# A channel-mix weight stored by column group, so that each decoded set of parts is one contiguous run

## The chip, the cores and the metric

The kernel runs on one core of one Trainium2 chip. The metric is device time in microseconds (us): three runs of the kernel before gave 630.12 to 631.0 us, with a median of 630.76 us. A core has five engines that run side by side and each take their instructions in order: TensorE (PE, with PEld for loading its stationary operand), VectorE (DVE), ScalarE (ACT), GpSimd (POOL) and SyncE (SP), which here issues all the DMAs.

## The reference

For four batches of 768 tokens, three stages follow each other.

```python
# 1. a decayed scan over time, 8 heads of width 48 (384 channels)
y[:, :, t] = einsum(r_t, state + einsum(u * k_t, v_t)); state = w_t * state + einsum(k_t, v_t)
# 2. causal attention of 4 experts (width 64), every expert computed, the best two of a token mixed
a = softmax(scale * q @ k.T, causal); out += gate * (a @ v @ wo[e])
# 3. layernorm and channel mix, w_ch1: 384 x 1536, w_ch2: 1536 x 384
ch = maximum(xn @ w_ch1, 0) @ w_ch2; return x + ch
```

The weights arrive as 64-bit floats and have to become 16-bit pairs on the chip (a high part, and a low part that holds the rest), so that a product is three matmuls of 16-bit operands.

## The kernel before

The scan is worked in six chunks of 128 tokens for a batch (names `seq`, `bw`, `fw`, `k`, `rp`, `am`, and on PE `pk`, `pa`, `pcb`, `pd`, `py`), the attention in six query tiles (`pq`, `pv`, `ps`, the transposed probabilities `pt`, `po`, `oT`, `px`), and the channel mix in three groups of 256 tokens for a batch (`xnT`, `pm` at L1532 with w_ch1, `hid`, `pz` at L1565 with w_ch2). Scan of batch b+1, attention of batch b and channel mix of batch b-1 or b are interleaved.

Weight `w1` (the first channel-mix weight, 384 rows) is held in a tile `w_w` of 12 parts of 128 x 384; before, part `4*kk + f` holds rows 128*kk and on, of column group f (KK = 3 row blocks, 4 column groups). `w2` has 12 parts as well. The parts are fetched in *sets*: three parts of w1 (one column group) or two of w2. For each set:

- a DMA (L552) brings the 64-bit words into a raw tile (`x` for w1, `xnT` for w2);
- DVE decodes them in three instructions to 32-bit floats, written over the place in `w_w` where the 16-bit pairs will stand: L505 (one source: shift and mask), L506 and L507 (two sources: the sign, then the low bits);
- ACT squares and sums them (L575, `top`), for the scales.

From the first set's sum the scales follow, and then each part goes through PE, ACT, PE, ACT: a product with a diagonal matrix that scales it (L655, `times`), its 16-bit high part written to `w_w` (L659, `hi`), that part subtracted in the accumulator (L663, `less`), and the rest written as the low part (L667, `lo`). Later sets of w2 instead go over ACT L632 and DVE L636.

In the old layout the three parts of a w1 set stand four apart: parts f, 4+f, 8+f. The decode reads and writes `full[:, pick]` with a stride of four parts, so that from the set's first element to its last lie parts of other sets.

The order is not that of the source. Each step is recorded as an operation with an engine, a length and its dependencies; a planner then sorts the operations of each engine by due numbers (sums of entries of the table `PLACE` by group, step and index) and emits them in that order. Semaphore waits are added afterwards by the framework, from which ranges of a tile instructions read and write. A few filler matmuls (L744, `spin`) are put in by the planner near the start, where PE would stand idle.

Of the kernel before, what the change touches and what calls it, by code (L numbers as in the profile page):

```python
# [20 lines left out]
P = 128  # L21
# [5 lines left out]
KK = DM // P  # L27
# [10 lines left out]
PRM = dict(LOOK=0.0, LATE=1773.6262, UNTIL=43.8356, SPAN=6.2999, LEAST=0.0732, GAP=2.1085, LAND=2.27, NPA=6, NQ=1, NCB=8, DIRECT=('w2',), NST=10)  # L38
PLACE = {
# [21 lines left out]
    ('o', 3, 5): -698477.53, ('proj', 0): -295018.27, ('proj', 0, 's'): -125022.81, ('proj', 0, 1): 80220.25,  # L61
    ('proj', 0, 2): -21343.01, ('proj', 1): -177643.56, ('proj', 1, 1): -107377.99, ('proj', 1, 2): -196040.46,
    ('proj', 2): -91098.53, ('proj', 2, 1): 13642.21, ('proj', 2, 2): -449346.82, ('proj', 3): 93391.83,
# [12 lines left out]
    ('vals', 0, 1): 35417.3, ('vals', 0, 2): -24875.8, ('vals', 1): -89872.89, ('vals', 2): 21146.28,  # L76
# [7 lines left out]
    ('w2', 8): 67189.64, 'a_den': -27933.93, 'a_hi': -151558.33, 'a_lo': 225945.59, 'a_of': -8012.47,  # L84
    'a_sum': 90213.0, 'a_tr': -81147.68, 'ae': 9532.96, 'am_copy': 126573.78, 'f_flag': -83856.37,
    'f_rows': 359040.86, 'f_turn': 39994.68, 'f_w': 28227.87, 'forth': 248281.69, 'g_exp': 19442.15,
    'g_norm': -38900.58, 'g_peak': -151938.75, 'g_rank': 230355.43, 'hi': 134007.83, 'less': -136319.44,
    'lo': -225283.24, 'load': -122866.37, 'load_g': -30043.72, 'load_k': -57046.71, 'load_q': -279458.56,
    'load_r': -217492.83, 'load_u': -13561.36, 'load_ut': 56724.36, 'load_v': 141804.62, 'm_hi': -262991.62,
    'm_lo': 122988.52, 'm_out': -32307.81, 'm_store': 132697.31, 'mk': 33523.95, 'mk_begin': 34263.89,  # L90
    'mk_bonus': -306653.38, 'mk_cb': -154529.96, 'mk_dec': -93213.35, 'mk_diag': -197725.73, 'mk_k2': 294244.16,
    'mk_k2t': 81775.2, 'mk_rk': -143861.49, 'mk_rp': -291319.24, 'mk_ruk': -96442.3, 'mk_sd': -340521.47,
    'mk_side': 120524.29, 'mk_tot': 228284.39, 'mm_1': 319489.06, 'mm_2': 191970.76, 'mm_a': -77276.6,
    'mm_av': -163565.22, 'mm_cb': 11831.02, 'mm_d': -269837.93, 'mm_inter': -24853.46, 'mm_intra': -48830.3,
    'mm_k': -8197.28, 'mm_o': 142200.91, 'mm_q': -177202.8, 'mm_s': -59954.25, 'mm_v': -130717.65, 'mt': -15383.65,
    'n_hi': -5943.82, 'n_lo': -146399.19, 'n_root': -31312.6, 'n_tr': 121898.14, 'n_var': -147654.16,
    'n_xn': -111826.26, 'o1': 140934.93, 'o2': -234884.57, 'o3': 6748.89, 'o4': -239856.13, 'o5': 93661.14,
    'o_mean': 273629.77, 'o_st': 120380.94, 'o_x1': -222100.87, 'q_hi': 140529.69, 'q_less': 98224.57,
    'q_lo': 97584.28, 's_bias': -108185.03, 's_exp': 5623.4, 's_hi': 119074.81, 's_lo': 11657.8, 's_max': 72228.32,
    's_tr': 53618.26, 'scan': 180273.48, 'se': -288101.94, 'stack_k': 117902.0, 'stack_q': 35533.64,  # L100
    'state': -226076.38, 'times': 63945.68, 'top': 19104.78, 'unpack': -157479.11, 'unpack2': 157371.31,
    'unpack3': 101864.41, 'v_hi': 188866.74, 'v_lg': -140728.23, 'v_lo': 25317.14, 'vc': -144449.83,
    'w_check': 22598.42, 'w_sane': 282903.73, 'ws_hi': 30208.09, 'ws_less': -128406.54, 'ws_lo': -66728.24,
# [200 lines left out]
NR = KK * DF // RW  # L304
# [1454 lines left out]
```

## Time and profile before

| | before |
|---|---|
| median of three runs | 630.76 us (630.12 to 631.0) |
| the profiled execution | 629.59 us |
| its span | 627.3 us, 16254 instructions |
| mean granted TensorE clock | 0.970 |
| PE busy | 598.3 us (95%) |
| DVE, ACT, POOL busy | 427.4, 386.0, 140.1 us |

The 2.3 us between the profiled execution and its span lie around the span and are not seen in the trace. PE is the engine of which the most is used; a stretch of the span can shorten only where PE stands idle or runs at the lower of its two clocks (1.2 GHz, written 0.5, and 2.4 GHz, written 1.0), and the rows below are chosen to show where that is.

### The profile page before, as it was taken

The numbers are of one execution on the slowest core, as the hardware profiler recorded it, in microseconds if no ns is written. First come the engines' busy times: TensorE is split into PE (matmuls) and PEld (weight loads), VectorE is DVE, ScalarE is ACT, GpSimd is POOL, SyncE is SP. The second block draws the span as 40 slices with busy tenths as digits, with TensorE's granted clock in tenths as the row PEclk, the third lists the DMA queues.
The fourth block names the chain that finished last, engine by engine and source line by source line (L and its number), as shares of the span: only waits on it lengthen the run. The fifth ranks groups of instructions, "written<-read, shape, count | busy, mean of one in ns | idle before, by whom it ended". The sixth has DMA issues, their size and how long they took to land.

```text
span 627.3 us, 16254 instructions
## 1 busy us (share of the span) xinstructions
PE 598.3 (95%) x6593; PEld 440.9 (70%) x6594; DVE 427.4 (68%) x808; ACT 386.0 (62%) x1062; POOL 140.1 (22%) x176
## 2 busy tenths in 40 slices
PE   6589899899999999999999999999999999999996
PEld 3357566677668866876877676776886768687783
DVE  5978788988978588888874898674464555542220
ACT  5367889876765586776656777573464756343120
POOL 4613043333644034325400232000000000000000
PEclk8659999899999999999999999999999999999999
DMA  8623764698996488739754767626228454522000
GB/s 279 228 101 124 191 168 128 130 226 212 193 215 123 93 217 162 186 81 248 168 84 103 194 128 162 112 56 121 48 43 152 93 102 85 100 62 60 14 14 31
DMA packets 150706, 82.15 MB, mean 131 GB/s; under 512 B 123616, under 2 KB 136672, under 8 KB 150624
## 3 DMA queue, kind: packets, MB, share of 16 engines
q1 hardware_dynamic: 150624, 81.03, 56.5%
q8 instruction: 54, 0.88, 0.6%
q14 instruction: 28, 0.23, 0.1%
HBM read 41.16 MB, written 4.72 MB: 73 GB/s over the span
## 4 chain that ended last, share of the span: by engine, by line
PE 72%; ACT 12%; DVE 10%; issue 3%; DMA 2%; SPq 0%; POOL 0%; ACTq 0%; DVEq 0%
PE pz L1565 21%; PE pm L1532 18%; PE pq L1123 7%; PE ps L1302 5%; PE po L1387 4%; PE px L1439 3%; ACT ps L1344 3%; PE pa L918 3%; PE py L968 2%; PE py L954 2%; PE pv L1188 1%; PE pk L936 1%; ACT hl L1360 1%; PE pd L983 1%; DMA xnT<-in_w_dram 1%
## 5 line engine op out<-in xcount | busy, mean ns | idle before, releaser
L1565 PE MATMUL pz<-w_w,hid 128*128 128x384 f16 x864 | 151.0, 326 | 0.2 <-DVE hid L1547 0.2
L1532 PE MATMUL pm<-xnT,w_w 128*128 128x256 f16 x1296 | 149.9, 273 | 0.2 <-DVE hid L1547 0.2
L1532 PEld LDWEIGHTS <-w_w 128*128 128x128 f16 x1296 | 124.8, 98 | 17.1 <-issue 1.7
L1565 PEld LDWEIGHTS <-hid 128*128 128x128 f16 x864 | 81.9, 98 | 50.7 <-issue 1.8
L1364 DVE SCALAR_TENSOR_TENSOR hl<-ps,hl 128x512 f16<-128x512 f32 (+2 forms) x68 | 54.7, 812 | 33.7 <-ACT hl L1360 33.0
L1547 DVE SCALAR_TENSOR_TENSOR hid<-pm,hid 128x512 f16<-128x512 f32 x72 | 49.3, 687 | 37.7 <-ACT hid L1543 37.6
L1543 ACT ACTIVATE hid<-pm 128x512 f16<-128x512 f32 x72 | 42.8, 594 | 50.8 <-PE pm L1532 50.7
L1481 POOL TENSOR_TENSOR rs_y<-rs_v,half 128x2 f32<-128x2 f32 x12 | 9.4, 780 | 229.6 <-ACT rs_v L1477 229.6
L1123 PE MATMUL pq<-xT,w_qk 128*128 128x256 f16 x432 | 51.8, 273 | 0.5 <-ACT qs L1148 0.5
L1360 ACT ACTIVATE hl<-ps 128x512 f16<-128x512 f32 (+2 forms) x68 | 46.7, 696 | 4.9 <-DMA pt<-hl 3.6
L1344 ACT ACTIVATE ps<-ps,bias 128x640 f32<-128x640 f32 (+1 forms) x32 | 26.2, 820 | 37.1 <-DVE ps L1315 34.1
L1123 PEld LDWEIGHTS <-w_qk 128*128 128x128 f16 x432 | 41.7, 98 | 6.9 <-issue 1.3
L891 POOL TENSOR_SCALAR_AFFINE_SELECT am<-cb 128x512 f32<-128x512 f32 x48 | 34.7, 745 | 40.2 <-DVE cb L877 26.2
L833 POOL TENSOR_TENSOR rp<-seq,fw 128x512 f32<-128x512 f32 x24 | 30.6, 1273 | 51.0 <-DVE fw L816 42.5
L1387 PEld LDWEIGHTS <-pt 128*128 128x128 f16 x1008 | 37.2, 99 | 5.6 <-DMA pt<-hl 1.0
L1387 PE MATMUL po<-vt,pt 128*128 128x64 f16 x1008 | 40.3, 194 | 0.6 <-DMA pt<-hl 0.5
L1572 DVE SCALAR_TENSOR_TENSOR x<-pz,ioutFalse,x 128x384 f32<-128x384 f32 x24 | 14.7, 614 | 36.7 <-PE pz L1565 36.7
L1315 DVE TENSOR_SCALAR_CACHE_REDUCE ps<-ps,scales 128x640 f32<-128x640 f32 (+1 forms) x32 | 30.6, 956 | 12.8 <-PE ps L1305 12.7
L1344 ACT ACTIVATE ps<-ps,bias,scales 128x128 f32<-128x128 f32 (+3 forms) x64 | 37.9, 591 | 1.8
L925 DVE COPY_PREDICATED am<-above,pa 128x512 f32<-128x512 int8 x48 | 33.0, 723 | 4.3 <-PE pa L918 4.2
L801 DVE TENSOR_TENSOR_SCAN bw<-seq,starts 128x516 f32<-128x516 f32 x24 | 30.9, 1288 | 1.5 <-DMA seq<-in_seq_dram 1.5
L918 PE MATMUL pa<-rp,k 48*128 48x128 f32 x384 | 29.6, 290 | 1.7 <-DVE dec L996 1.6
(225 smaller groups left out, 1060.0 us busy)
## 6 DMA issues: line engine op xcount, KB each, us to landing
seq<-in_seq_dram SPq DMA_DIRECT2D x48, 256.0 KB, 4.0
seq<-in_seq_dram SPq DMA_DIRECT2D x24, 258.5 KB, 3.3
tok<-in_tok_dram SPq DMA_DIRECT2D x16, 384.0 KB, 4.0
seq<-in_seq_dram SPq DMA_DIRECT2D x24, 192.0 KB, 4.0
xnT<-in_w_dram SPq DMA_DIRECT2D x6, 768.0 KB, 4.4
x<-in_w_dram SPq DMA_DIRECT2D x4, 1152.0 KB, 7.2
out_dram<-x SPq DMA_DIRECT2D x24, 192.0 KB, 2.6
xk<-kd SPq DMA_DIRECT2D x16, 192.0 KB, 4.2
```

Of the source, the lines that this page charges most:

```text
L891: G.affine_select(out=t["am"][:, j], in_=t["cb"].rearrange("p (h j) -> p h j", j=2)[:, :, j, None].to_broadcast([P, NP, P]), compare_op=OP ...
L918: T.matmul(t["pa"][j][:, hp * P : (hp + 1) * P], t["k2"][o : o + D, hp, :], t["rp"][o : o + D, hp, :], start=True, stop=True)
L925: V.copy_predicated(t["am"][:, j], above[:, None, :].to_broadcast([P, NP, P]), t["pa"][j].rearrange("p (h t) -> p h t", t=P))
L1123: T.matmul(h["pq"][:, :n].rearrange("p (c t) -> p c t", t=P), wt["qk"][:, lw, kk, mt * P : (mt + 1) * P], t["xT", c0 // 2][:, :, lx * KK + ...
L1344: A.activation(ps, ps, AF.Exp, bias=h["bias"][:, e : e + 1], scale=-1.0 if alone else t["x"]["esc"], accum_out=r["sums"][:, e : e + 1])
L1360: A.activation(part(u, heads, 0, W), view(heads, h, W, spot), AF.Copy, scale=2.0 ** 14)
L1364: V.scalar_tensor_tensor(out=part(u, heads, half_at, W), in0=view(heads, h, W, spot), scalar=2.0 ** 14, in1=part(u, heads, 0, W), op0=OP.m ...
L1387: T.matmul(r["po"][:, e * HD : (e + 1) * HD], u["pt"][:, (lp * len(heads) + k) * (i + 1) + kb, :], t["vt"][:, kb, lv, e * HD : (e + 1) * H ...
L1532: T.matmul(h["pm"][:, j * 256 : (j + 1) * 256].rearrange("p (c t) -> p c t", t=P), wt["w1"][:, 4 * kk + f // 3, lw, f % 3 * P : (f % 3 + 1 ...
L1543: A.activation(hid[fp][:, 0], h["pm"], AF.Relu)
L1547: V.scalar_tensor_tensor(out=hid[fp][:, 1], in0=h["pm"], scalar=0.0, in1=hid[fp][:, 0], op0=OP.max, op1=OP.subtract)
L1565: T.matmul(h["po"][:, :DM], hid[fp][:, lh, c0 : c0 + P], wt["w2"][:, 2 * fp + j, lw, :], start=(fp + j + i == 0), stop=(fp == NF // 2 - 1 ...
```

## The change

The parts of w1 are renumbered: part `KK*f + kk` now holds row block kk of column group f, so that the three parts of a set are neighbours. The decode's view of the tile becomes one run of 1152 elements; the DMA still fetches the same strided columns from the weight. Who indexes the tile by part is changed to match. Beside that the whole table of due numbers is set anew, of which two lines stand here.

```diff
-PRM = dict(LOOK=0.0, LATE=1773.6262, UNTIL=43.8356, SPAN=6.2999, LEAST=0.0732, GAP=2.1085, ...)
+PRM = dict(LOOK=0.0, LATE=4084.3652, UNTIL=54.3975, SPAN=7.4609, LEAST=0.218, GAP=1.7191, ...)
 PLACE = {
-    ('av', 0, 0): 47055.04, ('av', 0, 1): -203728.69, ('av', 0, 2): -46772.52, ('av', 0, 3): -134002.41,
+    ('av', 0, 0): 16836.1, ('av', 0, 1): -209210.03, ('av', 0, 2): -42671.94, ('av', 0, 3): -81935.9,
...
-    SETS = dict(w1=[[4 * kk + f for kk in range(KK)] for f in range(4)], w2=[[2 * j, 2 * j + 1] for j in range(NR // 2)])
+    SETS = dict(w1=[[KK * f + kk for kk in range(KK)] for f in range(4)], w2=[[2 * j, 2 * j + 1] for j in range(NR // 2)])
...
-                pick = slice(some[0], some[-1] + 1, some[1] - some[0])
+                pick = slice(some[0], some[-1] + 1)
+                src = slice(k, None, 4) if which == "w1" else pick
...
-                def load(pick=pick, flat=flat, ring=ring, hold=hold, n=n, direct=direct):
+                def load(pick=src, flat=flat, ring=ring, hold=hold, n=n, direct=direct):
...
-                    kk = part * KK // NR
+                    kk = part % KK
...
-                    T.matmul(hold["ps"], diags[which][:, part * KK // NR if which == "w1" else 0], full[:, part], start=True, stop=True)
+                    T.matmul(hold["ps"], diags[which][:, part % KK if which == "w1" else 0], full[:, part], start=True, stop=True)
...
-                @op("PE", 0.98, after=[q["ready"]] + [big_done["w1"][4 * kk + (2 * fp + j) // 3] for kk in range(KK)], follow=[mms[-1] if mms else pe],
+                @op("PE", 0.98, after=[q["ready"]] + [big_done["w1"][KK * ((2 * fp + j) // 3) + kk] for kk in range(KK)], follow=[mms[-1] if mms else pe],
...
-                                     wt["w1"][:, 4 * kk + f // 3, lw, f % 3 * P : (f % 3 + 1) * P], q["xnT"][:, :, lx * KK + kk, :],
+                                     wt["w1"][:, KK * (f // 3) + kk, lw, f % 3 * P : (f % 3 + 1) * P], q["xnT"][:, :, lx * KK + kk, :],
```

What the planner makes of it shows at three places. The lines of the changed kernel are one higher from L546 on.

On DVE, at the decode of the second set of w1 (`w_w_132` is w1, `w_w_133` w2, `x_69` and `xnT` their raw tiles), before:

```order
L505 TENSOR_SCALAR w_w_132<-x_69 128x3x384
L713 SCALAR_TENSOR_TENSOR w_vg<-raw_vg_165,s_all_False,w_vg 128x4
L506 SCALAR_TENSOR_TENSOR w_w_132<-x_69,w_w_132 128x3x384
L507 SCALAR_TENSOR_TENSOR w_w_132<-x_69,w_w_132 128x3x384
L506 SCALAR_TENSOR_TENSOR w_w_133<-xnT,w_w_133 128x768
```

and of the changed kernel at the same place:

```order
L505 TENSOR_SCALAR w_w_132<-x_69 128x1152
L714 SCALAR_TENSOR_TENSOR w_vg<-raw_vg_165,s_all_False,w_vg 128x4
L506 SCALAR_TENSOR_TENSOR w_w_132<-x_69,w_w_132 128x1152
L507 SCALAR_TENSOR_TENSOR w_w_132<-x_69,w_w_132 128x1152
L506 SCALAR_TENSOR_TENSOR w_w_133<-xnT,w_w_133 128x768
```

Nothing moved here; the written piece became one run.

On PE, where the fourth query tile of batch 0 is multiplied out (`po_3`, its third piece reading `pt_3_2`), before:

```order
L1532 MATMUL pm_0_4_1994<-xnT,w_w_132 128x256
L1387 LDWEIGHTS pt_3_2_1925
L1387 MATMUL po_3_1854<-vt_715,pt_3_2_1925 128x64
...
L1387 MATMUL po_3_1854<-vt_715,pt_3_2_1925 128x64
L979 MATMUL pd_2_2022<-dec_102,ident 128x384
L983 MATMUL pd_2_2022<-seq_2_1666,k2t_2_1989 48x48 x8
L1387 LDWEIGHTS pt_3_3_1953
```

and now:

```order
L1533 MATMUL pm_0_4_1998<-xnT,w_w_132 128x256
L980 MATMUL pd_2_2014<-dec_102,ident 128x384
L984 MATMUL pd_2_2014<-seq_2_1670,k2t_2_1993 48x48 x8
L1388 LDWEIGHTS pt_3_2_1929
L1388 MATMUL po_3_1858<-vt_719,pt_3_2_1929 128x64
```

The nine `pd_2` matmuls moved from behind the third piece of `po_3` to ahead of it.

On SP's queue, at the last query tile of batch 1 (`pt_5_...` are transposes of its probabilities, `seq_3` and `tok_3` the inputs of a scan chunk of batch 3), before:

```order
L1373 DMA_TRANSPOSE pt_5_1_4778<-hl_5_1_4740 128x12x128
L1373 DMA_TRANSPOSE pt_5_2_4857<-hl_5_2_4819 128x12x128
L1428 DMA_TRANSPOSE oT_4_4888<-o_1_4_4754 128x4x128
L1373 DMA_TRANSPOSE pt_5_3_4935<-hl_5_3_4908 128x12x128
L1428 DMA_TRANSPOSE oT_5_5056<-o_1_5_5045 128x4x128
```

and now:

```order
L1374 DMA_TRANSPOSE pt_5_1_4788<-hl_5_1_4744 128x12x128
L773 DMA seq_3_4883<-in_seq_dram 128x517
L797 DMA tok_3_4891<-in_tok_dram 128x768
L1374 DMA_TRANSPOSE pt_5_2_4896<-hl_5_2_4847 128x12x128
L781 DMA seq_3_4883<-in_seq_dram 128x512
L785 DMA seq_3_4883<-in_seq_dram 128x512
L1429 DMA_TRANSPOSE oT_4_4928<-o_1_4_4754 128x4x128
L789 DMA seq_3_4883<-in_seq_dram 128x384
L1374 DMA_TRANSPOSE pt_5_3_4975<-hl_5_3_4941 128x12x128
```

Five input loads moved from behind the whole tile to between its transposes. From here to the attention of batch 3 the orders of PE, ACT, DVE and SP differ in many places; ahead of here they differ in few.

## Rows read from the trace of the kernel before

**Rows 1.** The head of the page.
```profile
span 627.3 us, 16254 instructions
```

**Rows 2.** Stretches: us, busy PE, PEld, DVE, ACT, POOL (count), clock, DMA, GB/s.
```profile
0.00:45.00 45.00, 30.38 (x213) 18.50 (x215) 35.29 (x79) 22.61 (x78) 19.94 (x31) 0.66 0.59 195
45.00:150.00 105.00, 97.21 (x1135) 69.08 (x1134) 90.49 (x164) 87.83 (x260) 31.75 (x35) 0.98 0.69 171
150.00:615.00 465.00, 463.61 (x5207) 349.21 (x5204) 300.40 (x564) 275.52 (x726) 88.38 (x111) 1.00 0.56 118
```

**Rows 3.** Line 505: duration min/median/max in ns, first and last start, forms.
```profile
L505 DVE TENSOR_SCALAR w_w<-xnT x6: 551/627/984, 15.1 to 111.1; 128x768 int32<-128x768 int32 x6
L505 DVE TENSOR_SCALAR w_w<-x x4: 1340/1344/1348, 21.2 to 74.3; 128x1152 int32<-128x1152 int32 x4
```

**Rows 4.** Timeline of the second w1 set: start, length, instruction, [idle before, releaser].
```profile
34.80 1.19 POOL L833 TENSOR_TENSOR rp<-seq,fw 128x512 f32<-128x512 f32 x1 [4.09 <-DVE fw L816]
...
35.42 1.34 DVE L505 TENSOR_SCALAR w_w<-x 128x1152 int32<-128x1152 int32 x1
...
37.45 1.35 DVE L506 SCALAR_TENSOR_TENSOR w_w<-x,w_w 128x1152 int32<-128x1152 int32 x1
38.09 1.06 PE L725 MATMUL ws_ps<-raw_qk,sd 128*128 128x256 f32 x2
...
38.89 0.49 ACT L659 ACTIVATE w_w<-w_ps_False 128x384 f16<-128x384 f32 x1 [0.76 <-DVE w_w L506]
...
39.42 1.36 DVE L507 SCALAR_TENSOR_TENSOR w_w<-x,w_w 128x1152 int32<-128x1152 int32 x1 [0.62 <-ACT w_w L659]
...
40.83 0.48 PE L663 MATMUL w_ps_False<-w_w,minus 128*128 128x384 f16 x1 [1.68 <-DVE w_w L507]
```

**Rows 5.** Pieces of the chain that ended last: start, length, what.
```profile
41.31 1.44 PE py L968 x24
...
43.17 1.27 PE w_ps_False L655 x2
...
54.45 0.79 PE py L968 x24
...
88.07 0.65 PE w_ps_False L655 x2
```

**Rows 6.** Busy time and granted clock in four short stretches, columns as in rows 2.
```profile
39.00:41.00 2.00, 0.32 (x2) 0.00 (x0) 1.58 (x2) 0.66 (x2) 0.00 (x0) 0.50 0.00 0
...
44.00:45.00 1.00, 0.55 (x3) 0.15 (x2) 0.00 (x0) 0.47 (x2) 0.00 (x0) 1.00 0.76 262
113.00:115.00 2.00, 0.43 (x7) 0.46 (x9) 1.95 (x5) 1.98 (x4) 0.00 (x0) 1.00 1.03 202
116.00:119.00 3.00, 3.00 (x30) 2.37 (x28) 3.00 (x4) 3.00 (x8) 0.72 (x1) 0.50 0.56 190
```

**Rows 7.** Timeline at the fourth w1 set, columns as in rows 4.
```profile
75.69 0.49 ACT L659 ACTIVATE w_w<-w_ps_False 128x384 f16<-128x384 f32 x1 [0.66 <-PE py L954]
...
77.78 0.32 PE L663 MATMUL w_ps_False<-w_w,minus 128*128 128x384 f16 x1 [0.19 <-DVE w_w L506]
...
79.24 0.49 ACT L1002 ACTIVATE spare<-py 128x384 fp8e4<-128x384 f32 x1
```

**Rows 8.** Timeline at the third w1 set, POOL beside DVE.
```profile
54.80 2.34 POOL L891 TENSOR_SCALAR_AFFINE_SELECT am<-cb 128x512 f32<-128x512 f32 x2
54.93 1.71 DVE L506 SCALAR_TENSOR_TENSOR w_w<-x,w_w 128x1152 int32<-128x1152 int32 x1
```

**Rows 9.** PE's waits up to 150 us: us in total, times, longest.
```profile
PE po L1387 <- DMA pt<-hl: 0.5, 1, 0.5
```

**Rows 10.** The tile `pt`, written by transposing DMAs: time to landing.
```profile
DMA to landing us min/median/max: 3.0/3.8/6.5
```

**Rows 11.** Timeline at the end of batch 1's last query tile.
```profile
325.11 1.42 SPq L1373 DMA_TRANSPOSE pt<-hl  x1
...
330.14 0.70 PE L1387 MATMUL po<-vt,pt 128*128 128x64 f16 x18
```

More of the change, by code (lines that the diff above doesn't have):

```diff
@@ L36 @@
 PACK = OFF_TV + DM
-PRM = dict(LOOK=0.0, LATE=1773.6262, UNTIL=43.8356, SPAN=6.2999, LEAST=0.0732, GAP=2.1085, LAND=2.27, NPA=6, NQ=1, NCB=8, DIRECT=('w2',), NST=10)
+PRM = dict(LOOK=0.0, LATE=4084.3652, UNTIL=54.3975, SPAN=7.4609, LEAST=0.218, GAP=1.7191, LAND=2.27, NPA=6, NQ=1, NCB=8, DIRECT=('w2',), NST=10)
 PLACE = {
[21 rows of a table removed]
-    ('o', 3, 5): -698477.53, ('proj', 0): -295018.27, ('proj', 0, 's'): -125022.81, ('proj', 0, 1): 80220.25,
-    ('proj', 0, 2): -21343.01, ('proj', 1): -177643.56, ('proj', 1, 1): -107377.99, ('proj', 1, 2): -196040.46,
-    ('proj', 2): -91098.53, ('proj', 2, 1): 13642.21, ('proj', 2, 2): -449346.82, ('proj', 3): 93391.83,
[12 rows of a table removed]
-    ('vals', 0, 1): 35417.3, ('vals', 0, 2): -24875.8, ('vals', 1): -89872.89, ('vals', 2): 21146.28,
[7 rows of a table removed]
[L84 to L103, printed above, removed]
-    'ws_load': 66852.66, 'ws_times': -17374.3, 'ws_top': -348457.17, 'x_hi': -14285.97, 'x_lo': 26889.45,
-    'x_rest': -61247.9, 'xabs': -182346.53,
[21 rows of a table added]
+    ('o', 3, 5): -702290.43, ('proj', 0): -300762.99, ('proj', 0, 's'): 3258.44, ('proj', 0, 1): 93098.76,
+    ('proj', 0, 2): -21532.93, ('proj', 1): -194846.79, ('proj', 1, 1): -182281.63, ('proj', 1, 2): -206567.32,
+    ('proj', 2): -139967.36, ('proj', 2, 1): -60620.28, ('proj', 2, 2): -471991.76, ('proj', 3): 33470.28,
[12 rows of a table added]
+    ('vals', 0): -221914.55, ('vals', 0, 1): 9510.27, ('vals', 0, 2): -3038.04, ('vals', 1): -123387.73,
[8 rows of a table added]
+    'a_hi': -190161.82, 'a_lo': 255406.1, 'a_of': -1740.35, 'a_sum': 77515.98, 'a_tr': -87884.88, 'ae': 27221.68,
+    'am_copy': 109115.04, 'f_flag': -61865.24, 'f_rows': 383190.12, 'f_turn': 50312.51, 'f_w': 27951.92,
+    'forth': 229228.26, 'g_exp': 45423.87, 'g_norm': -61796.84, 'g_peak': -154339.3, 'g_rank': 221135.62,
+    'hi': 130307.72, 'less': -133603.61, 'lo': -226558.93, 'load': -122063.24, 'load_g': -63513.62,
+    'load_k': -47163.22, 'load_q': -260808.06, 'load_r': -213091.8, 'load_u': -988.12, 'load_ut': 54846.76,
+    'load_v': 150565.96, 'm_hi': -311237.37, 'm_lo': 98927.68, 'm_out': 48881.52, 'm_store': 128283.34,
+    'mk': 37503.41, 'mk_begin': 79557.08, 'mk_bonus': -282399.21, 'mk_cb': -133359.0, 'mk_dec': -110093.06,
+    'mk_diag': -221089.1, 'mk_k2': 283945.41, 'mk_k2t': 74583.4, 'mk_rk': -113571.57, 'mk_rp': -253737.39,
+    'mk_ruk': -124526.78, 'mk_sd': -316789.73, 'mk_side': 122534.0, 'mk_tot': 231221.44, 'mm_1': 365622.4,
+    'mm_2': 204989.47, 'mm_a': -89716.58, 'mm_av': -132220.31, 'mm_cb': -32343.06, 'mm_d': -271848.69,
+    'mm_inter': -12262.99, 'mm_intra': -28587.77, 'mm_k': -8994.31, 'mm_o': 164809.69, 'mm_q': -178559.25,
+    'mm_s': -93850.65, 'mm_v': -174740.15, 'mt': -29113.63, 'n_hi': -30793.97, 'n_lo': -156027.19,
+    'n_root': -62676.59, 'n_tr': 158968.05, 'n_var': -141023.27, 'n_xn': -89663.96, 'o1': 157478.1, 'o2': -192466.52,
+    'o3': -11415.96, 'o4': -238836.12, 'o5': 57587.18, 'o_mean': 330064.88, 'o_st': 128824.23, 'o_x1': -246691.1,
+    'q_hi': 91258.53, 'q_less': 155281.43, 'q_lo': 90976.99, 's_bias': -147965.71, 's_exp': 22959.99,
+    's_hi': 126955.2, 's_lo': 15768.81, 's_max': 97591.03, 's_tr': 93388.25, 'scan': 169869.4, 'se': -267199.41,
+    'stack_k': 101409.78, 'stack_q': 52977.27, 'state': -243711.11, 'times': 65418.22, 'top': 39150.99,
+    'unpack': -128317.31, 'unpack2': 202491.49, 'unpack3': 98913.69, 'v_hi': 168006.56, 'v_lg': -190314.23,
+    'v_lo': 35276.99, 'vc': -154269.88, 'w_check': 55447.28, 'w_sane': 274698.76, 'ws_hi': 45782.35,
+    'ws_less': -112839.4, 'ws_lo': -48993.3, 'ws_load': 19982.66, 'ws_times': -17264.02, 'ws_top': -282259.34,
+    'x_hi': -423.83, 'x_lo': 17645.98, 'x_rest': -65141.57, 'xabs': -200566.42,
```

79 rows, old and new, of the table PLACE are left out of this document.

## The prediction

> **What bounds the kernel now.** I read the profile in four steps: the table of stretches, the chain that ended last, the timeline around the places where that chain passes through the weight decode, and the list of what PE waited for.
>
> The stretches come first. From 150 to 615 us PE is busy 463.61 of 465.00 us at the full clock [rows 2]: whatever happens there on DVE or ACT, at most 1.4 us can be won. Up to 45 us PE is busy 30.38 us and its granted clock is 0.66; from 45 to 150 it is busy 97.21 of 105 us [rows 2]. So 14.6 + 7.8 = 22.4 us of idle PE, and the slow clock, lie in the first 150 us of a span of 627.3 us [rows 1]. This is where w1 and w2 are decoded, and where a change to the decode can pay.
>
> In the chain the second w1 set is seen as a zigzag between 37 and 41 us; the timeline gives it [rows 4]. PE has finished its first scaling product (L655) and goes on with L725 until 39.15. ACT L659 could write the high part of that first part, but starts only at 38.89, after 0.76 idle, released by DVE's L506. DVE L507 then waits 0.62 us for ACT L659, and PE's L663 waits 1.68 us for DVE L507, with every other PE instruction queued behind it. Yet these belong to different sets: L659 and L663 work on a part of the first set, L506 and L507 on the second. What ties them is the place in the tile: before, the decoded parts of a set are four parts apart, and between its first and last element lie parts of the others. The same pattern stands at 75 us: ACT L659 begins at 75.69 after 0.66 idle (DVE's last L505 of w1 had started at 74.3 and ran 1.34, so it ended just then, though the row names an older PE event), and PE L663 waits 0.19 us for DVE L506 [rows 3, 7].
>
> **The change part by part.**
>
> *The ties between sets.* With a set in one run, nothing of another set lies inside the range that its decode touches; L659 then waits only for its own product, L663 only for L659, L507 only for L506. At 37 to 41 us: L655 stands on PE ahead of L725, which starts at 38.09, and ACT sat idle for 0.76 us before 38.89; so L659 can end by about 38.7, before PE's L725 ends at 39.15. L663 can follow at 39.15 instead of 40.83: 1.68 us [rows 4]. What is late next? The next scaling product needs L507 of the second set, now done at 38.80 + 1.36 = 40.2, while PE reaches that product at 43.17 - 1.68 = 41.5 [rows 4, 5]. So nothing takes the place of the wait. Everything behind it on PE, the release of scan inputs to SP included, moves with it.
>
> The clock widens this. The granted clock is 0.50 in 39 to 41 us and 1.00 from 44 on; PE was idle 1.68 of the 2 us at 39, and from 40.83 on had worked without a pause when it rose [rows 6]. Without the pause PE works on from before 37 us. If the clock then rises when the pause would have ended, the 24 `py` matmuls take 0.79 instead of 1.44 us and two L655 0.65 instead of 1.27 [rows 5]: 1.3 us more. If it rises at the same 44 us, what was done in the first 1.7 us of full clock is now done at half speed; with PE busy 0.55 us of that first us [rows 6] this takes back about 1. So the term lies between 0.7 and 3.0 us. I take 2.2: the hole itself, and 0.5 for a somewhat earlier rise, since the row before the rise is one without a pause.
>
> At 75 us: ACT L659 starts up to 0.66 earlier, PE L663 0.19 earlier. ACT's L1002 at 79.24 needs the `py` matmuls that PE runs behind L663 [rows 7], so of the 0.66 only PE's 0.19 passes this point. Bounds 0 and 0.66, taken: 0.2, the nearer row.
>
> *The access shape of L505.* Four instructions take 1340 to 1348 ns for 1152 elements. The six of w2 go over 768 elements in one run, at best in 551 ns [rows 3]. By that rate 1152 take 551 x 1152/768 = 0.83 us: 0.5 us less each, 2.1 us of DVE in all. I count none of it. At the first set DVE waits next for ACT; at the second, L507 is no longer what PE waits for (40.2 against 41.5, above); the third set's sums come long after; at the fourth, ACT's `py` work stands behind it. Bounds: 0, and 1.0 if the second and fourth still lay on the chain. L506 and L507 have two sources; I leave them at their 1.35 us [rows 4].
>
> The Trainium skill has a rule on this, and one against it. "VectorE: DVE Perf Modes", section "Mode 2×_2P", says that a one-source instruction takes two elements a cycle when the outermost dimensions of source and destination are both even or equal: 3 against 1152 fails, 1152 against 1152 passes. "SBUF — State Buffer", section "Who interferes with whom", says that in this mode DVE and GpSimd exclude each other for a whole instruction. The trace bears both out: the w2 ones spread from 551 to 984 ns, and DVE's L506 took 1.71 us beside a POOL L891, against 1.35 [rows 3, 4, 8]. By that rule the second set's L505 would wait for POOL's L833, which runs from 34.80 to 35.99, and end at 36.8, as now; the sum by it is the same, since I count nothing for L505.
>
> *The table.* Up to 150 us it moves little. Two more spins go where PE stands idle. The `pd_2` matmuls now stand ahead of the third piece of `po_3`, for which PE waits 0.5 us for a DMA [rows 9]; `pd_2`, one product of 128 x 384 and eight small ones, fills that. Bounds 0 (another operand late) and 0.5, taken: 0.3. From the last query tile of batch 1 on (the 320s) the orders differ, but PE is full there and the sum of its matmuls is the same; bounds: a gain of 1.4 us at most, a loss priced below; taken: 0.
>
> *Sum.* 2.2 + 0.2 + 0.3 = 2.7 us of the profiled execution's 629.59, that is 626.9. Its span is 627.3; the 2.3 us around it do not change. It ran 1.2 us under the median of the runs shown, to which I apply the difference: 630.76 - 2.7 = 628.1.
>
> **The rivals.**
>
> *Given back.* From 45 to 150 us DVE is busy 90.49, ACT 87.83 of 105 us, and the mean DMA share is 0.69 [rows 2]. If the scan chain on DVE or the transfers, not PE, set the pace up to 150 us, an earlier PE only waits longer. For it: both engines are nearly as full as PE. Against it: scan inputs and weights are released by the very PE work that moves up, and the DMAs stand nearly still at 39 to 41 us [rows 6]. Then some 0.5 us is left: 630.3.
>
> *A second clock gain.* PE idles 1.57 us at 113 to 115 and the clock falls to 0.50 in 116 to 119, with PE busy all 3 us [rows 6]. If the shift closes that pause, 1.5 us more: 626.6.
>
> *Slower, by the new order.* On SP's queue five loads of `seq_3` and `tok_3` now stand between the transposes of batch 1's last query tile, the first of them waiting for PE work on an earlier chunk. Before, the last transpose was issued at 325.11, its `po` ran at 330.14 with no wait [rows 11]: 5.0 us for a landing of 3.8 at the median and 6.5 at the longest [rows 10]. If it lands at the longest, and is held behind the loads for as much again (2 x 2.7 us), it comes 5.4 us later than the median; 1.2 us are in hand, so PE waits 4.2 us, and a pause at 113 us was followed by a fall of the clock that cost half of 3 us [rows 6]. Against it: by PE's new order 81 matmuls of `pq` and `pz` stand between the scores of that tile and this `po`, 72 before, so it is also needed a little later. 628.1 + 4.2 + 1.5 = 633.8. It decides from a landing 3.7 us later than the median (a pause of 2.5 us and the clock's 1.5 are the 2.7 won and 1.3 more); below that the change is not slower.
>
> *That it doesn't do what it says.* If the ties are not by place, L663 still waits 1.68 us for L507; what is left is the L505 rate and `pd_2`: 630.3. The rows speak against it, since L659 waits for an L506 whose data it does not use.
>
> **How the numbers follow.** Forecast 0.52; the second clock gain 0.13; given back, or the ties stay, 0.22; slower 0.13. About 0.2%, 1.26 us, is what a measurement of this kernel tells from no change, so faster means below 629.5, slower above 632.0. Faster 0.52 + 0.13 = 0.65, same 0.22, slower 0.13. The likeliest case's own range is 626.6 to 629.5 (all its terms at their upper bounds, 3.0 + 0.66 + 0.5, to the 1.26 us that can be told). The range reaches 625.8 below, into the second clock gain, and 631.0 above, over the case that it is given back.
>
> **What would show it.** In the changed profile L505 of w1 takes about 0.8 us where POOL rests; ACT L659 waits for PE, not for L506; PE L663 at 39 us has no wait; PE is busy in 39 to 41 us, and the clock is 1.00 before 44. The scaling product after it starts by 41.5. From 150 us PE's waits stay near 1.4 us in sum. Wrong would be: the scaling product still at 43.1, PE idle grown between 90 and 150 us by what was won, or a wait of `po` for `pt` at 325 to 335 us.

## The result, and the profile after

The changed kernel ran in 625.62 us (median of five runs, 624.05 to 626.54) against 630.76 us (629.95 to 631.57): a ratio of 0.9919, 95% interval 0.9900 to 0.9938, 5.1 us faster. The forecast was 628.1 us and the range began at 625.8. The direction was right; the size fell 0.2 us below the range. Measured again on another chip, the ratio was 0.9935 (0.9909 to 0.9961), 626.52 against 629.90 us, 3.4 us faster. Single runs of the unchanged kernel on one chip spread from 627.55 to 634.98 us, and by the intervals the gain lies between 3.9 and 6.3 us in the first measurement and between 2.5 and 5.7 us in the second: neither the 5.1 nor the 3.4 is exact to 1 us.

The profiled execution took 625.62 us with a span of 623.2, against 629.59 and 627.3 [rows 1]: 4.0 and 4.1 us less. That pair of traces is what can be taken apart.

The three stretches of the changed kernel (columns as in [rows 2], which they answer):

```profile
0.00:45.00 45.00, 35.08 (x234) 21.62 (x236) 35.28 (x80) 25.01 (x85) 19.80 (x32) 1.00 0.65 218
45.00:150.00 105.00, 98.03 (x1183) 70.55 (x1182) 92.38 (x167) 88.22 (x263) 33.22 (x37) 0.98 0.66 165
150.00:615.00 465.00, 462.94 (x5166) 348.88 (x5165) 299.50 (x561) 272.18 (x716) 87.40 (x109) 1.00 0.57 118
```

In the first 45 us PE now runs 234 matmul records where it ran 213; what PE does in each later stretch comes earlier. The place of the second w1 set, answering [rows 4] (the last line stands a little later):

```profile
34.54 1.18 POOL L834 TENSOR_TENSOR rp<-seq,fw 128x512 f32<-128x512 f32 x1 [4.08 <-DVE fw L817]
...
35.16 1.17 DVE L505 TENSOR_SCALAR w_w<-x 128x1152 int32<-128x1152 int32 x1
...
36.38 1.65 PE L656 MATMUL w_ps_False<-w_w,diag_w_False 128*128 128x384 f32 x2
...
38.07 0.49 ACT L660 ACTIVATE w_w<-w_ps_False 128x384 f16<-128x384 f32 x1 [0.22 <-PE w_ps_False L656]
38.61 0.32 PE L664 MATMUL w_ps_False<-w_w,minus 128*128 128x384 f16 x1
...
38.86 1.36 DVE L507 SCALAR_TENSOR_TENSOR w_w<-x,w_w 128x1152 int32<-128x1152 int32 x1
...
40.37 0.88 PE L656 MATMUL w_ps_False<-w_w,diag_w_False 128*128 128x384 f32 x2 [0.42 <-DVE w_w L507]
...
42.41 0.32 PE L664 MATMUL w_ps_False<-w_w,minus 128*128 128x384 f16 x1 [1.05 <-ACT w_w L660]
```

ACT L660 is released by PE, no longer by DVE's L506; L664 has no wait; L507 starts straight behind L506. The ties by place are gone. New are the last two rows. PE comes so early to the second L656 that it waits 0.42 us for L507, now a true dependency. Behind it PE waits 1.05 us for ACT, where the kernel before waited 0.53:

```profile
45.08 0.32 PE L663 MATMUL w_ps_False<-w_w,minus 128*128 128x384 f16 x1 [0.53 <-ACT w_w L659]
```

So about 0.9 us of what PE gained up to there is handed back to DVE and ACT.

Line 505, answering [rows 3] (duration min/median/max in ns):

```profile
L505 DVE TENSOR_SCALAR w_w<-xnT x6: 548/556/982, 15.8 to 108.3; 128x768 int32<-128x768 int32 x6
L505 DVE TENSOR_SCALAR w_w<-x x4: 747/1006/1744, 21.1 to 71.6; 128x1152 int32<-128x1152 int32 x4
```

The w1 instruction went from a steady 1340 to 1348 ns to 841, 1172, 1744 and 747 ns for the four sets. The shortest is where POOL rests; the longest stands beside POOL work:

```profile
50.47 1.55 POOL L834 TENSOR_TENSOR rp<-seq,fw 128x512 f32<-128x512 f32 x1 [4.29 <-PE ws_ps L734]
50.89 1.74 DVE L505 TENSOR_SCALAR w_w<-x 128x1152 int32<-128x1152 int32 x1
...
52.13 2.70 POOL L892 TENSOR_SCALAR_AFFINE_SELECT am<-cb 128x512 f32<-128x512 f32 x2
```

Here the "faster" form is 0.4 us slower than the old one. In both places where POOL's L834 had started first, at 35.16 and at 50.89, L505 ends 0.6 us after L834 does: it seems to await that end. The Trainium skill's "SBUF — State Buffer", section "Who interferes with whom", has the rule that of GpSimd and DVE in a two-port mode (the 2×_2P that the prediction names is one) the one that starts first blocks the other for its whole instruction. The trace agrees, with the two ends 0.6 us apart both times.

To see where the 4.1 us lie, each matmul of the kernel before is paired with the same one after (the k-th of its form), and the difference of their starts from the span's start is taken; the table has the median of each stretch, by time in the kernel before, minus is earlier. It holds all the kernels that follow. Past 300 us the order differs and only the end is comparable.

| us | 35 to 40 | 50 to 60 | 80 to 85 | 100 to 105 | 130 to 140 | 151 to 155 | 580 to 600 |
|---|---|---|---|---|---|---|---|
| changed kernel | -0.26 | -2.67 | -3.28 | -2.84 | -2.89 | -3.50 | -3.77 |
| the same, again | -0.16 | -2.41 | -3.03 | -2.60 | -2.72 | -3.50 | -4.14 |
| layout alone | -0.45 | -2.80 | -3.34 | -3.36 | -1.82 | -1.66 | -0.89 |
| order alone | -0.45 | +0.40 | +0.40 | +0.78 | +1.71 | +0.93 | +0.64 |
| two-source L505 | -0.72 | -2.52 | -2.94 | -2.50 | -1.24 | -2.02 | -2.83 |
| before, pause filled | -0.31 | -1.00 | -1.06 | -0.67 | +0.55 | +0.60 | +0.59 |
| layout and pd_2 | -0.66 | -3.07 | -3.69 | -3.25 | -3.08 | -3.93 | -4.10 |
| pd_2 put back | -0.12 | -2.53 | -3.17 | -2.72 | -2.73 | -2.75 | -3.45 |
| more spins | -0.04 | -2.43 | -3.00 | -2.56 | -2.70 | -3.47 | -4.03 |
| before, pd_2 moved | +0.37 | +0.14 | +0.09 | +0.49 | +1.94 | +1.09 | +0.79 |

Read along the first row: 2.41 us are won between 35 and 50, 0.17 net up to 105, 0.61 at 148, some 0.3 after 155, and the rest of the 4.1 before 35 us and behind the last matmul. Each row is one execution of its kernel.

### The profile page after: what moved, and what is told of

It is laid out like the page before. It is cut to its first block, busy times and chain, and to the rows that moved or that the text cites. A ratio compares the mean times of both kernels' runs of the same rounds, so it can differ in the third digit from the quotient of the medians.

```text
span 623.2 us, 16253 instructions
## 1 busy us (share of the span) xinstructions
PE 599.4 (96%) x6596; PEld 442.8 (71%) x6596; DVE 427.8 (69%) x808; ACT 385.4 (62%) x1062; POOL 140.4 (23%) x176
## 4 chain that ended last, share of the span: by engine, by line
PE 74%; ACT 10%; DVE 8%; DMA 4%; issue 2%; SPq 1%; POOL 0%; DVEq 0%; ACTq 0%
PE pm L1533 20%; PE pz L1566 19%; PE pq L1124 6%; PE ps L1303 5%; PE po L1388 4%; PE pa L919 3%; PE px L1440 3%; PE pv L1189 3%; ACT ps L1345 2%; PE py L955 2%; PE py L969 2%; DVE hl L1365 2%; ACT hl L1361 1%; DMA seq<-in_seq_dram 1%; DMA xnT<-in_w_dram 1%
## 5 line engine op out<-in xcount | busy, mean ns | idle before, releaser
L892 POOL TENSOR_SCALAR_AFFINE_SELECT am<-cb 128x512 f32<-128x512 f32 x48 | 35.4, 760 | 46.4 <-DVE cb L878 29.4
L834 POOL TENSOR_TENSOR rp<-seq,fw 128x512 f32<-128x512 f32 x24 | 30.8, 1285 | 50.2 <-DVE fw L817 38.6
L863 POOL TENSOR_TENSOR tok<-tok 128x384 f32<-128x384 f32 x16 | 19.4, 1211 | 72.6 <-DMA tok<-in_tok_dram 72.3
L802 DVE TENSOR_TENSOR_SCAN bw<-seq,starts 128x516 f32<-128x516 f32 x24 | 31.5, 1312 | 3.0 <-DMA seq<-in_seq_dram 3.0
```

The costliest lines, as they stand in the source:

```text
L802: V.tensor_tensor_scan(t["bw"][:, NP * CW : 0 : -1], t["wT"][:, NP * CW : 0 : -1], starts[:, NP * CW : 0 : -1], 0.0, op0=OP.mult, op1=OP.max)
L892: G.affine_select(out=t["am"][:, j], in_=t["cb"].rearrange("p (h j) -> p h j", j=2)[:, :, j, None].to_broadcast([P, NP, P]), compare_op=OP ...
```

## The experiments

Theory A: the ties between sets were the loss, and the pause's end (with the clock) is the gain. Theory B: the new order carries it. The times are medians of seven or twelve runs, against the kernel before on the same chip.

**Layout alone.** The changed kernel with the old table of due numbers, its w1 entries renumbered to the new parts; PE, DVE and ACT then run the old order, instruction for instruction.

```diff
-PRM = dict(LOOK=0.0, LATE=4084.3652, UNTIL=54.3975, ...)      # and the new PLACE
+PRM = dict(LOOK=0.0, LATE=1773.6262, UNTIL=43.8356, ...)      # and the old PLACE, ('w1', i) renumbered
```

> The new layout of w1 with the old order, instruction for instruction. Theory A (the ties between sets go, the pause of PE at 39 us closes and the clock rises earlier): PE's L664 at 39 us waits for ACT L660 alone, the matmuls behind it run 2.4 to 2.7 us earlier, and nearly all of that stays: span some 2.7 us shorter than before (624.6), ratio 0.9957. Theory B (the order carries the gain): under 0.7 us shorter, ratio 0.999 or more.

Measured: 627.65 us against 630.35, ratio 0.9954 (0.9935 to 0.9973), where theory A had 0.9957. In its trace L664 has no wait, with the old order of every engine, and the matmuls from 50 us on run 2.80 us earlier, 2.35 of it between 35 and 50 (table):

```profile
38.43 0.32 PE L664 MATMUL w_ps_False<-w_w,minus 128*128 128x384 f16 x1
```

Theory A holds; B, which allowed 0.7, does not. One expectation was missed: nearly all of it was to stay, but this execution loses 1.5 us again between 105 and 130 and has a span of 626.1 us, not 624.6. The next run shows where.

**Order alone.** The kernel before with the new table, renumbered the other way.

```diff
-PRM = dict(LOOK=0.0, LATE=1773.6262, UNTIL=43.8356, ...)      # and the old PLACE
+PRM = dict(LOOK=0.0, LATE=4084.3652, UNTIL=54.3975, ...)      # and the new PLACE, ('w1', i) renumbered
```

> The new order with the old layout of w1. Theory A: the pause of 1.7 us at 39 us and the tie at 75 us stay; only pd_2 at 148 us (0.6), the late stretch (0.2) and the end (0.3) are won: span 1.0 to 1.4 us shorter than before, ratio 0.998. Theory B: 3 us or more shorter, ratio 0.995 or less. If the two add up, e1's and e2's gains sum to the changed kernel's 4.1 us of span.

Measured: 630.47 against 630.35 us, ratio 0.9993 (0.9974 to 1.0012): nothing that can be told, less than the 1.0 to 1.4 expected. The trace shows why they don't add up: the pd_2 step is there (+1.71 to +0.93), but it is paid for twice. The first place is the pause (-0.45 to +0.40), which the old layout leaves in. PE in the timeline, and the stretches around it:

```profile
40.36 0.32 PE L663 MATMUL w_ps_False<-w_w,minus 128*128 128x384 f16 x1 [2.03 <-DVE w_w L507]
...
41.94 1.65 PE L655 MATMUL w_ps_False<-w_w,diag_w_False 128*128 128x384 f32 x2
```

```profile
36.00:39.00 3.00, 2.33 (x12) 1.33 (x9) 2.38 (x6) 2.23 (x9) 0.79 (x2) 0.70 0.00 0
39.00:42.00 3.00, 1.64 (x34) 1.00 (x33) 2.97 (x3) 1.44 (x3) 0.00 (x0) 0.87 0.00 0
42.00:45.00 3.00, 2.57 (x7) 1.24 (x6) 0.82 (x3) 2.29 (x8) 0.00 (x0) 0.50 0.75 234
```

Here the clock had risen before the pause and fell again behind it: 0.50 in 42 to 45, and L655 takes 1.65 us. The kernel before with only pd_2 moved, below, shows the same (0.98 in 39 to 42, 0.50 in 42 to 45). So the pause has a second price in two of the four executions with the old layout: the clock fell again behind it.

The second place is at 118 us (+0.78 to +1.71 between 105 and 130). DVE's scan L801 takes 2.20 us here, and PE then waits 1.16 us for DVE's `hl` behind it; in the changed kernel the same scan (L802) takes 1.21. Order alone, then the changed kernel:

```profile
118.63 1.28 POOL L847 TENSOR_TENSOR rk<-seq 128x512 f32<-128x512 f32 x1 [4.81 <-DMA seq<-in_seq_dram]
118.79 2.20 DVE L801 TENSOR_TENSOR_SCAN bw<-seq,starts 128x516 f32<-128x516 f32 x1
```

```profile
115.19 1.21 DVE L802 TENSOR_TENSOR_SCAN bw<-seq,starts 128x516 f32<-128x516 f32 x1
115.32 2.14 POOL L848 TENSOR_TENSOR rk<-seq 128x512 f32<-128x512 f32 x1 [5.12 <-DMA seq<-in_seq_dram]
```

Whichever of the two starts clearly first keeps its length, and the other is the longer by 0.6 to 1.0 us. POOL's product starts when the DMA of `seq` has landed. In four executions it came first, and the scan took 1.94 (layout alone), 2.20 (order alone), 2.23 (pause filled) and 1.79 us (before, pd_2 moved): these are four of the five rows of the table that lose 0.9 us or more between 105 and 130. In the other seven the scan took 1.21 or 1.22 us. No run was made to set which comes first, so why it falls out as it does stays open.

**L505 kept slow.** The changed kernel, with the first decode step of w1 as a two-source instruction of the same values.

```diff
+    ones30 = const.tile([P, 1, 1], I32, name="ones30")
+    G.memset(ones30, 0x3FFFFFFF)
...
-        return (lambda: V.tensor_scalar(d, hi, 3, 0x3FFFFFFF, op0=OP.logical_shift_left, op1=OP.bitwise_and),
+        first = (lambda: V.tensor_scalar(d, hi, 3, 0x3FFFFFFF, op0=OP.logical_shift_left, op1=OP.bitwise_and))
+        if d.shape[1] == KK:
+            first = (lambda: V.scalar_tensor_tensor(out=d, in0=hi, scalar=3, in1=ones30.to_broadcast([P, KK, RW]), op0=OP.logical_shift_left, op1=OP.bitwise_and))
+        return (first,
```

> The changed kernel with w1's L505 written as a two-source instruction (a mask in a tile as second source, the same values), so that it runs at one element a cycle as before, some 1.35 us. Theory A (nothing of L505's rate reaches PE but what L507 hands to the second L656, for which PE waited 0.42 us): 0 to 0.6 us longer than the changed kernel, ratio to before 0.992 to 0.993. Rival (the faster decode is a part of the gain that the sum left out): 1 us or more longer, ratio 0.9935 or more.

Measured: ratio 0.9952 (0.9931 to 0.9973), beside 0.9919 and 0.9935 of the changed kernel: by the medians the rival's number, but the intervals overlap. The source line of L505 here:

```profile
L510 DVE SCALAR_TENSOR_TENSOR w_w<-x,ones x4: 1348/1608/2345, 20.6 to 71.9; 128x1152 int32<-128x1152 int32 x4
```

It is slower than the old form too (up to 2345 ns beside POOL). In the trace it costs 0.15 us at 50 to 60 us in the absolute, 0.6 counted from 35 us on (table); another 1.3 us are lost between 105 and 130, where the clock is 0.50 all the way from 112 to 118 us (in the changed kernel 0.69 in 112 to 116) and the scan keeps its 1.22 us. So L505's rate is worth some tenths up to 60 us, and whether the rest belongs to it stays open.

**The pause filled, not removed.** The kernel before, with four filler matmuls into an unused accumulator.

```diff
+        done = 0
         for o in self.order(look, late, warm):
+            if warm and o.run.__name__ == "less":
+                if done == 0:
+                    for _ in range(4):
+                        warm["fill"]()
+                done += 1
             o.run()
...
+    def fill():
+        T.matmul(bank("o", "spin"), ident16, ballast, start=True, stop=True)
```

> The kernel before with four filler matmuls put on PE in the pause at 39 us, directly ahead of L663; nothing else is changed, so L663 still waits for L507. If the earlier rise of the clock is a gain of its own beside the closed pause: the py matmuls after 41 us run at full speed and the rest 0.5 to 0.8 us earlier, span 626.6. If the clock does not rise earlier without the rest of the change, or the work behind is bound otherwise: the same time as before, within 0.2 us of span.

Measured: 629.40 against 630.35 us, ratio 0.9986 (0.9963 to 1.0008): not to be told by time. Its stretches:

```profile
36.00:39.00 3.00, 2.83 (x14) 1.72 (x12) 2.47 (x5) 2.24 (x10) 0.92 (x2) 0.50 0.00 0
39.00:42.00 3.00, 2.57 (x37) 1.29 (x37) 2.88 (x3) 1.38 (x4) 0.00 (x0) 0.89 0.00 0
42.00:45.00 3.00, 2.10 (x7) 0.89 (x8) 1.55 (x3) 3.00 (x10) 0.00 (x0) 1.00 0.73 219
```

The clock rose within 39 to 42 us, where before it stayed at 0.50 up to 44 [rows 6], and the matmuls behind run 0.7 us earlier (-0.31 to -1.00) though L663 still waits for L507. I take this as the clock's share of the 2.4 us, and the 1.7 that are left as the pause's, by subtraction between two kernels. What was won is lost again between 105 and 130 in this execution, 1.0 of it where DVE's scan took 2.23 us; its span was 627.6, not the 626.6 expected.

**The piece of order at 148 us**, tried three ways: added to the layout alone, taken out of the changed kernel, and added to the kernel before.

```diff
+        out = self.order(look, late, warm)
+        if warm:
+            d = next(o for o in out if o.run.__name__ == "mm_d" and o.terms[0][0] == ("rw", 8))
+            av = next(o for o in out if o.run.__name__ == "mm_av" and o.terms[:2] == [(("av", 0, 3), 1.0), ("ae", 2)])
+            out.remove(d)
+            out.insert(out.index(av), d)        # put back: out.index(av) + 1
...
```

> The new layout with the old order, and of the new order one piece alone: the pd_2 matmuls of batch 1 ahead of the third piece of po_3. If that piece is worth what the traces show at 148 us: 0.6 to 0.75 us of span less than the new layout alone, and no wait of po for pt there; ratio 0.9945. If it is eaten further on: the same as the layout alone, 0.9954.

> The changed kernel with the pd_2 matmuls of batch 1 put back behind the third piece of po_3. The wait of 0.5 us for the transposed piece comes back; 0.6 to 0.75 us more than the changed kernel. If the rest of the new order has moved the transposes so that nothing waits there: no difference.

> The kernel before, old layout and old order, with one piece moved: the pd_2 matmuls of batch 1 ahead of the third piece of po_3. If that piece stands by itself, as with the new layout: PE's 0.5 us wait of po for pt goes and the matmuls from 149 us on run 0.6 to 0.75 us earlier, to the end; ratio 0.999. If it pays only once the layout has brought PE ahead of the transposing DMAs: no difference at 150 us.

Measured: layout and pd_2 626.19 us, ratio 0.9927 (0.9899 to 0.9955); the changed kernel on the same chip 626.52, put back 627.40 (0.9959, 0.9935 to 0.9984), all against 629.90. Before with pd_2 moved: 630.26 against 630.45 (0.9991, 0.9970 to 1.0012). The times alone leave it unclear; the table does not: between 130 and 151 us every kernel with the move gains (0.61, 0.78, 0.78, 0.78, 0.85, 0.77, 0.85), and every one without stays within 0.2. The three timelines of PE: layout alone, layout and pd_2, and put back.

```profile
146.69 0.52 PE L1388 MATMUL po<-vt,pt 128*128 128x64 f16 x12 [0.76 <-DMA pt<-hl]
```

```profile
144.50 0.81 PE L986 MATMUL pd<-dec,ident 128*128 128x384 f32 x2
145.24 0.56 PE L990 MATMUL pd<-seq,k2t 128*48 128x48 f32 x16
145.74 0.87 PE L1394 MATMUL po<-vt,pt 128*128 128x64 f16 x24
```

```profile
145.59 0.52 PE L1394 MATMUL po<-vt,pt 128*128 128x64 f16 x12 [0.50 <-DMA pt<-hl]
```

With the move there is no wait, and both pieces of `po` run in one go; without it the wait is back, 0.50 and 0.76 us. The move needs nothing of the layout. It is worth more than the 0.5 us of the wait's row [rows 9]: some 0.8. The kernel before shows where the rest is:

```profile
148.34 0.41 PEld L1387 LDWEIGHTS <-pt 128*128 128x128 f16 x12 [0.77 <-DMA pt<-hl]
148.34 0.52 PE L1387 MATMUL po<-vt,pt 128*128 128x64 f16 x12 [0.50 <-DMA pt<-hl]
```

PE's idle time is counted from the end of the matmul ahead, the last `pm`, which started at 147.57 and is taken to last 0.27 us. But matmuls overlap: in the kernel before with pd_2 moved, the next one starts 0.11 us after the last `pm` (149.41 and 149.52). From start to start the wait costs 0.77 - 0.11 = 0.66 us, not 0.50. Another 0.08 us is won between the two 128x384 products of `pd_2`, whose starts lie 0.41 us apart before and 0.33 with the move. Together that is 0.74 of the 0.75 us by which the stretch from the last `pm` to the first `py` is shorter (2.90 and 2.15 us).

**More fillers, to beat both.** The changed kernel with eight more, where PE is idle at 18, 28 and 31 us.

```diff
+        more = {20: 3, 25: 4, 27: 1} if warm else {}     # PE operation: fillers ahead of it
...
+                for _ in range(more.get(n, 0)):
+                    warm["fill"]()
```

> The changed kernel with eight more filler matmuls on PE where it stands idle: three ahead of the first py at 18 us, four ahead of L435 at 28 us, one ahead of L446 at 31 us. If PE's half clock up to 40 us still costs: the clock rises before 34 us, pd, L656 and L726 run at full speed there, and 0.5 to 1.5 us are won beyond the changed kernel (0.990). If DVE, busy nearly without a break from 15 to 41 us, bounds this stretch: within 0.3 us of the changed kernel, or slower where a filler is late.

Measured: 627.09 us, ratio 0.9953 (0.9932 to 0.9975), beside 626.52 of the changed kernel on the same chip; in the table it is where the changed kernel is from 50 us on. Nothing won, which is what was expected if DVE sets the pace up to 40 us. But the fillers did not do what they were put in for: the granted clock is still 0.50 in 30 to 36 us and 0.72 in 36 to 39. Whether a faster clock would pay there was therefore not tested. No version tried beats the changed kernel; layout with the pd_2 piece alone can't be told from it (626.19 and 626.52 us).

> The changed kernel once more, on the chip of the next three. If layout and order simply add up (0.9954 and 0.9993 of before), its ratio is about 0.995; if the first measurement holds, 0.992, and layout and order are worth more together than apart.

The second measurement, 0.9935, lies between the two numbers, and its interval holds the first.

## Why the prediction was right in kind and short in size

- *The ties between sets.* Right, and right in size: 2.2 us forecast (bounds 0.7 and 3.0), 2.41 measured from 35 to 50 us, the same within 0.2 in every kernel with the new layout and the fast L505. One line was off: I had PE reach the second L656 at 41.5, after L507's end. With the clock up it was there before, and L507, at 40.2 as worked out, became the next bound for 0.42 us, and ACT behind it for 0.5 us more than before.
- *The set at 75 us.* 0.2 forecast; 0.6 by 85 us in the changed kernel, of which 0.44 is given back at 85 to 90 (in the layout alone it is kept until 105). Net 0.17. The tie is gone: ACT L660 no longer waits for DVE, and PE's L664 has no wait.

```profile
72.23 0.48 ACT L660 ACTIVATE w_w<-w_ps_False 128x384 f16<-128x384 f32 x1
...
74.56 0.33 PE L664 MATMUL w_ps_False<-w_w,minus 128*128 128x384 f16 x1
```

- *L505.* The rate came as the row of w2 said (0.75 where POOL rests, forecast 0.83), but beside POOL most of it is lost: the four instructions save 0.87 us of DVE in all, where 2.1 was worked out. Counting nothing for PE was near, too low by some tenths. The prediction also counted L506's 1.71 us beside POOL [rows 8] as bearing out the rule for one-source instructions; L506 has two sources, so that row doesn't speak to it.
- *pd_2: the term that was mis-sized, and the step that failed.* I took 0.3 within bounds of 0 and 0.5, the length of PE's wait. It was 0.6 to 0.85 in seven executions: the row of a wait is not the upper bound that I made of it. From start to start the wait cost 0.66 us, and 0.08 more came between the products of `pd_2` (above).
- *The order from batch 1's last tile on.* Taken at 0; kernels with the new order gain 0.3 to 0.8 us between 155 and 600 us, the old order from 0.3 gained to 0.8 lost, so about half a us was missed. No run takes this piece by itself. The slower rival, built on the loads between the transposes, did not come: from 150 to 615 us PE waited 2.0 us in all (near 1.4 was forecast), none of it for `pt`:

```profile
PE ps L1303 <- DVE hl L1365: 1.6, 4, 0.5
PE pk L937 <- DVE k L829: 0.4, 1, 0.4
```

- *From the execution to the median.* The sum was made against an execution of 629.59 us and set against a median of 630.76. Between the profiled executions 4.0 us were won (2.7 forecast), between the first medians 5.1. A range built only of the terms' bounds left out how far a median of a few runs of this kernel lies from another: 5.1 and 3.4 us for the same pair of kernels. With pd_2 at 0.8 and 0.5 for the late order the sum would have been 3.7, 627.1 us. The 0.2 us by which the first median lies below the range is less than the two medians differ by, and the second one, 626.52, lies inside. That it does is no merit of the range: its lower end was drawn down to 625.8 for the second clock gain, which did not come.
- *The second clock gain.* It fell as a rival by its own mechanism. In the changed kernel the clock fell in 112 to 116 us; in its second execution it did not, and nothing was won. First the one, then the other execution, the stretches, and of the second the matmul that shows why:

```profile
112.00:116.00 4.00, 4.00 (x45) 3.32 (x44) 4.00 (x6) 3.97 (x10) 0.68 (x1) 0.69 0.69 235
```

```profile
112.00:116.00 4.00, 3.82 (x50) 3.19 (x51) 4.00 (x6) 3.97 (x10) 0.51 (x1) 1.00 0.69 231
116.00:118.00 2.00, 0.57 (x7) 0.28 (x6) 1.96 (x5) 1.97 (x8) 1.86 (x2) 1.00 0.01 4
```

```profile
117.47 0.82 PE L1303 MATMUL ps<-kd,qs 64*128 64x512 f16 x6 [1.43 <-DVE hl L1365]
```

Without the fall PE is done earlier and waits 1.43 us for DVE's `hl`; with it PE is done just in time. The start of that product is 117.30 with the fall and 117.47 without it. I had priced the slow clock by PE's busy time alone.

## What to carry to other kernels

In this kernel dependencies were drawn from the range that an instruction's access pattern spans: a strided view of a shared tile tied together instructions that share no data, and showed in the profile as a wait for a releaser whose output the waiting instruction does not read. Look for such rows first; here one cost about 1.7 us and the clock with it about 0.7. Price a pause of PE from start to start of its matmuls, not by the idle time in the row: 0.66 us against 0.50 here. The slow clock at 112 to 116 us cost nothing, because PE was not the last to arrive, so look behind a slow stretch for the wait that takes its place; and when the claimed gain is under 1% of a kernel whose single runs spread as much, take it apart by pairing instructions between traces, and give the range the spread of the medians too.

## What had not been expected of the hardware

- The granted clock of an execution can be missing from its records. In the changed kernel's first 45 us it stands at 1.00 throughout, yet L656 at 36.38 took 1.65 us, as L655 does at 0.50, and 0.88 at 40.37. There the duration of a known matmul tells the clock, not the column.
- The fast form of L505 beside POOL is slower than the plain one: 1744 ns against 1348, with POOL's own L892 pair at 2.70 us where before it took 2.34 [rows 8].
- Where the clock falls differs between executions of one program: in the changed kernel it stood at 0.69 in 112 to 116 us, in that kernel's second execution at 1.00. In the layout alone it fell earlier (0.57 in 106 to 110).
- What is lost between 105 and 130 us is not mainly the clock's. Of the 1.5 us in the layout alone (table: -3.36 to -1.82) 0.7 are DVE's scan at 1.94 us instead of 1.21; the rest is lost ahead of it, where the clock was low. With the order alone and with the pause filled the scan's 1.0 us covers all or most of it. There the scan or POOL's product was lengthened, whichever had started second.
